# Attention with a feed-forward block behind it: the first feed-forward product begins 11 slots behind the scores instead of 13

## The chip, the cores and the metric

The kernel runs on one core of one Trainium2 chip. The core has five engines that run beside each other, each through its own instructions in order: TensorE (PE, matmuls; PEld is its weight load), VectorE (DVE), ScalarE (ACT), GpSimd (POOL) and SyncE (SP), which in this kernel issues all DMA transfers. They wait for each other through semaphores. The metric is the time of one execution in device microseconds (us), lower is better. The kernel before took 1484.6 us (median of 3 runs, 1483.02 to 1485.44).

## The reference

Attention over 8 batches, 12 heads, 448 positions and a head size of 64, and behind it a feed-forward block with a squared ReLU over the 3584 positions (width 768, inner width 2048). All arrays are float32, or float64 that is read as two words.

```
q_n = q / sqrt(mean(q*q) + 1e-6) * g_q          # k likewise with g_k
scores = q_n @ k_n.T / sqrt(64)
e = exp(scores - max(scores));  attn = e / (sum(e) + 1e-9)
x = attn @ v                                    # heads side by side: 768 columns
h = x @ w_in;  g = s * max(h, 0)**2 + b
out = g @ w_out
```

## The kernel before, in words

**Slots.** The 96 heads are taken as 48 pairs, 6 pairs to a batch. A pair takes 8 slots (two heads, four chunks of keys each), so there are 384 slots, 48 to a batch, and pair p begins in slot 8p. One Python loop walks the slots, and the order in which it emits instructions is the order in which each engine runs them. In slot s TensorE computes the transposed scores of chunk s (L407, L410), the plain scores of chunk s+10 (L369), from which VectorE takes the row maximum (`maximum`, L380), and weighs the values with chunk s-2 (`weigh`, L466). ScalarE takes the exponential of chunk s (L422 or L426), and from pair 12 on it rounds it to a high part (`split_e`, L434), of which VectorE makes the low part of chunk s-1 (`split_e_lo`, L447, tile `al`). The last matmul of a weighing reads that low part. Up to pair 11 the exponential stays in one part and L447 does not occur.

**Fill.** Between these matmuls, six in each slot, stand the matmuls of the first feed-forward product (FFN1) of the batch before (`ffn_in`, L182): 288 matmuls, so exactly 48 slots. They begin START slots after the batch's own 48: with START = 13 the FFN1 of batch 0 fills slots 61 to 108, that of batch 1 slots 109 to 156, and so on. Slots 0 to 60 have no fill. Behind slot 383 the loop runs on for the rest of the fill of batch 6; the FFN1 of batch 7 and the second product (FFN2, L707) follow without attention beside them.

**The way of the sums.** A ones column beside the values makes TensorE deliver the sum of the exponentials with the weighted values. For pair p, counted from its first slot: `take` (slots 6 and 10, ACT L475) copies the result out of PSUM, `gather` (slots 7 and 11, a DMA of 1.8 KB, L483) turns the row of sums into the tile `zt`, `invert` (slot 13, DVE L489 and L490) takes the reciprocal, `divide` step 1 (slot 14) writes it to DRAM, step 2 (slot 16) reads it back onto 64 partitions per head (`zb`), step 3 (slot 18, POOL L507, two instructions) multiplies and leaves the tile `u`. `split_x(b, k)` then rounds `u` of pairs 2k and 2k+1 of the batch into the high part of `x` (ACT L515) and takes the low part (DVE L516): two casts and two subtractions in each of three successive slots, the last of which is the first slot of that batch's fill.

**What stands around it.** `jobs[s]` lists for each slot what else is emitted: loading and normalising q and k of later pairs (L306, L311, L314, L315), scaling them (`scale`, POOL L331 and DVE L332, in slots 1 and 5 of a pair), splitting them (`split_kq`, ACT L350 and L351 in slots 3 and 7, POOL L353 and L354 a slot later), splitting the values (L299, L300). The first nine pairs take another way: rows are normalised and turned on TensorE (`turn`), then split (`split_turned`, ACT L255 to L257 and DVE L259, L260). Functions in `late` (`convert` and `invert`) come at the end of a slot, behind `maximum`. `convert` turns the float64 weights w_in into two float32 parts (ACT L128, L138; DVE L127, L130, L132, L135; POOL L141), piece by piece in slots up to 92. SyncE issues the DMAs in the order of emission too, and waits in that order.

Of the kernel before, what the change touches and what calls it, by code (L numbers as in the profile page):

```python
# [20 lines left out]

LEAST = (1 + 1 / 8) * 2.0 ** (0x70 - 127)

START = 13

AHEAD = 10

# [10 lines left out]
def attention_then_relu2_ffn(  # L38
# [38 lines left out]
    NP = NPAIR // B  # L77
# [15 lines left out]
    W = 8  # L93
# [117 lines left out]
    with tc.tile_pool(name="apool", bufs=1) as ap:  # L211
# [343 lines left out]
        def filler(n):  # L555

            for _ in islice(fill, n):
                pass
# [4 lines left out]
        def at(s_, f, *a):  # L563
            jobs[s_].append((f, a))

        for p in range(NPAIR):
            s0 = W * p
            if p >= NR:
                at(s0 - 32, load, p)
                at(s0 - 28, norm, p)  # L570
                at(s0 - 24, keep, p)
            for j in range(2):
                s1 = s0 + 4 * j
                if p >= NR:
                    at(s1 - 19, load_kq, p, j)
                    at(s1 - 19, spread, p, j)
                    at(s1 - 15, scale, p, j)
                    at(s1 - 13, split_kq, p, j)
                else:
                    at(max(s1 - 28, FIRST), load_rows, p, j)  # L580
                    at(s1 - 20, norm_rows, p, j)
                    at(s1 - 13, turn, p, j)
                    at(s1 - 12, split_turned, p, j)
                at(s1 - 10, double_kb, p, j)
                at(s1 - 6, shift, p, j)
                at(s1 + 6, take, p, j)
                at(s1 + 7, gather, p, j)
            at(s0 - (9 if p >= NV else 5), load_v, p)
            if p >= NV:
                at(s0 - 3, split_v, p)  # L590
            at(s0 + 13, invert, p)
            at(s0 + 14, divide, p, 1)
            at(s0 + 16, divide, p, 2)
            at(s0 + 18, divide, p, 3)
        for b in range(B):
            for k_ in range(3):
                at(W * NP * (b + 1) + START - 2 + k_, split_x, b, k_)
        for _ in range(2):
            at(FIRST + 1, load_piece)
        for s_ in PACE:  # L600
# [12 lines left out]
        with tc.manual_schedule(engines=ORDERED):  # L613
            begun = []
            for s_ in range(FIRST, NSLOT + START + 1):
                if s_ == FIRST:
# [37 lines left out]
                filler(FILL[2])  # L654
                b, m = divmod(s_ + 1 - START, W * NP)
                if m == 0 and b > 0:
# [151 lines left out]
```

## Time and profile before

| | |
|---|---|
| median of 3 runs | 1484.6 us (1483.02 to 1485.44) |
| profiled execution, its own time | 1483.03 us |
| its span (first to last instruction) | 1481.2 us |
| mean granted TensorE clock | 0.997 of full speed |
| busy: PE, PEld | 1443.3 us (97%), 1322.6 us (89%) |
| busy: DVE, ACT, POOL | 862.8 us (58%), 790.5 us (53%), 686.9 us (46%) |

The 1.8 us between the span and the execution's own time lie outside the program's instructions. The shares are means over stages: VectorE is near full in the first 180 us and far from it afterwards. In the 40 slices of the page, TensorE's busy share is 7 tenths in the first slice, 8 in the fourth and the last, and 9 or more in all others.

### The profile page before, as it was taken

Reading aid. Unit: us, or ns where it says so; the run is one execution under the profiler, and the core shown is the slowest. Engines: PE = TensorE matmul, PEld = TensorE weight load, DVE = VectorE, ACT = ScalarE, POOL = GpSimd, SP = SyncE. Lnnn points to the kernel's source line nnn. Section 1 sums busy time; section 2 is a strip of 40 time slices with the busy share of each in tenths; the row PEclk is TensorE's granted clock in tenths of the full one; section 3 lists DMA queues with packets and bytes.
Section 4 is the critical chain, followed back from the end, with each engine's and each line's share of the span. In section 5 each row is a group of like instructions: output and inputs, shape, how many; then the busy total and the mean of one; then the engine's idle time right before and its main releaser. Section 6 shows DMA issues by size and latency. Waiting matters only on the chain. (4 is left out here: it accounts for less than half of the span.)

```text
span 1481.2 us, 21369 instructions
## 1 busy us (share of the span) xinstructions
PE 1443.3 (97%) x7332; PEld 1322.6 (89%) x7332; DVE 862.8 (58%) x1328; ACT 790.5 (53%) x1445; POOL 686.9 (46%) x563
## 2 busy tenths in 40 slices
PE   7998999999999999999999999999999999999998
PEld 6665788899899899899899889999999999999998
DVE  7999996766766666766766664389522222222210
ACT  5777556766766666766766766456322222222210
POOL 7788887777677777777677763100000000000000
PEclk8999999999999999999999999999999999999999
DMA  5456876566666666566666652387333333233200
GB/s 141 130 159 183 233 219 203 171 196 186 188 190 184 189 192 185 170 199 191 188 175 198 189 171 58 118 273 242 105 97 85 96 94 78 79 91 106 79 22 32
DMA packets 218172, 225.31 MB, mean 152 GB/s; under 512 B 77936, under 2 KB 195696, under 8 KB 218064
## 3 DMA queue, kind: packets, MB, share of 16 engines
q1 hardware_dynamic: 218064, 223.95, 51.7%
q8 instruction: 58, 0.95, 0.3%
q14 instruction: 50, 0.41, 0.1%
HBM read 171.71 MB, written 40.82 MB: 143 GB/s over the span
## 5 line engine op out<-in xcount | busy, mean ns | idle before, releaser
L182 PE MATMUL ph<-x,wih 128*128 128x448 f32 x1536 | 490.0, 366 | 1.8 <-DVE x L516 1.8
L182 PEld LDWEIGHTS ph<-x,wih 128*128 128x128 f32 x1536 | 288.7, 188 | 31.7 <-issue 6.4
L380 DVE TENSOR_REDUCE nmx<-sh 112x1 fp32r<-112x448 f32 x384 | 237.0, 620 | 130.7 <-PE sh L369 127.7
L182 PE MATMUL ph<-x,wil 128*128 128x448 f32 x768 | 293.8, 383 | 0.0
L426 ACT ACTIVATE st<-st 128x448 f32<-128x448 f32 (+1 forms) x288 | 151.2, 525 | 220.3 <-PE st L410 213.6
L707 PE MATMUL po<-woh,gh 128*128 128x384 f32 x896 | 228.1, 334 | 0.3 <-ACT r L199 0.3
L707 PE MATMUL po<-wol,gh 128*128 128x384 f32 x896 | 227.9, 334 | 0.0
L707 PE MATMUL po<-woh,gl 128*128 128x384 f32 x896 | 227.7, 334 | 0.0
L466 PE MATMUL av<-ah,vs 128*128 128x448 f32 x576 | 164.3, 366 | 0.1
L369 PE MATMUL sh<-ka,qa 128*112 128x448 f32 x384 | 147.3, 386 | 16.0 <-DVE ka L259 10.9
L707 PEld LDWEIGHTS po<-woh,gh 128*128 128x128 f32 x896 | 161.9, 188 | 0.7 <-ACT r L199 0.6
L707 PEld LDWEIGHTS po<-wol,gh 128*128 128x128 f32 x896 | 161.9, 188 | 0.0
L707 PEld LDWEIGHTS po<-woh,gl 128*128 128x128 f32 x896 | 161.7, 188 | 0.0
L407 PE MATMUL st<-qa,ka 128*128 128x448 f32 (+1 forms) x384 | 159.2, 415 | 1.7 <-ACT e L422 0.8
L182 PEld LDWEIGHTS ph<-x,wil 128*128 128x128 f32 x768 | 144.3, 188 | 17.8 <-issue 6.9
L434 ACT CAST ah<-st 128x448 fp32r<-128x448 f32 (+1 forms) x288 | 153.9, 534 | 1.8
L447 DVE TENSOR_TENSOR al<-st,ah 128x448 fp32r<-128x448 f32 x216 | 132.4, 613 | 35.4 <-ACT ah L434 21.6
L689 ACT ACTIVATE r<-r 128x2048 f32<-128x2048 f32 x28 | 53.7, 1919 | 172.7 <-DMA r<-r_d 172.7
L410 PE MATMUL st<-qb,kb 128*128 128x448 f32 (+1 forms) x384 | 140.2, 365 | 0.0
L690 DVE TENSOR_SCALAR r<-r,sb_s,sb_b 128x2048 f32<-128x2048 f32 x28 | 37.6, 1346 | 173.2 <-ACT r L689 173.2
L507 POOL TENSOR_TENSOR u<-uz,zb 64x448 f32<-64x448 f32 x96 | 115.4, 1203 | 41.4 <-DMA zb<-z_d 27.7
L369 PEld LDWEIGHTS sh<-ka,qa 128*112 128x112 f32 x384 | 107.5, 281 | 28.9 <-ACT wih L138 4.7
(75 smaller groups left out, 2142.1 us busy)
## 6 DMA issues: line engine op xcount, KB each, us to landing
kq<-in_dram SPq DMA_DIRECT2D x78, 448.0 KB, 4.9
rb<-i_d SPq DMA_DIRECT2D x78, 448.0 KB, 5.9
r_d<-r SPq DMA_DIRECT2D x128, 224.0 KB, 2.8
r<-r_d SPq DMA_DIRECT2D x24, 1024.0 KB, 5.9
raw<-in_dram SPq DMA_DIRECT2D x39, 448.0 KB, 5.1
w64i<-in_dram SPq DMA_DIRECT2D x24, 512.0 KB, 4.9
w64o<-in_dram SPq DMA_DIRECT2D x32, 384.0 KB, 4.7
kb<-ka SPq DMA_DIRECT2D x96, 112.0 KB, 3.1
```

The lines of the kernel that those rows point to most:

```text
L182: T.matmul(ph[:, :SEQ], w[:, cc, f0 : f0 + P], xs[b, cc][:, part, :], start=n == 0, stop=n == 3 * NCC - 1,)
L369: T.matmul(sh[:QC, :SEQ], qa[p % 2][:, a].rearrange("k (p c) -> k c p", c=NQ)[:, c], ka[p % 2][:, a], start=True, stop=True,)
L380: V.tensor_reduce(out=nmxs[p][:, c : c + 1], in_=sh[:QC, :SEQ], op=ALU.max, axis=AX.X, negate=True)
L407: T.matmul(st[:rows, :SEQ], ka[n][:, keys], qa[n][:, q], start=True, stop=False)
L410: T.matmul(st[:rows, :SEQ], kb[n][:, keys], qb[n][:, q], start=False, stop=True,)
L426: S.activation(st[:rows, :SEQ], st[:rows, :SEQ], AF.Exp)
L434: S.copy(ah[:rows], sts[i][0][:rows, :SEQ])
L447: V.tensor_tensor(al, st[:rows, :SEQ], ah[:rows].bitcast(F32), ALU.subtract)
L466: T.matmul(av[:, :SEQ], x, a, start=kc == 0 and m == 0, stop=kc == 3 and m == len(todo) - 1,)
L507: G.tensor_tensor(u[a], uzs.pop((p, j))[a], zb[a], ALU.mult)
L689: S.activation(r, r, AF.Square)
L707: T.matmul(po[e][0][:, :HALF], x[:, fc, :], w[:, f, e * HALF : (e + 1) * HALF], start=fc == 0 and m == 0, stop=fc == NFC - 1 and m == 2,)
```

## The change

START goes from 13 to 11: the FFN1 of batch b fills slots 48(b+1)+11 to 48(b+1)+58, two slots earlier, and the loop ends two slots earlier. `split_x` goes with it, since its slots are counted from START. `invert` and the three steps of `divide` come one slot earlier in each pair (12, 13, 15, 17 instead of 13, 14, 16, 18); `take` and `gather` stay. For batch 0 alone, `split_x` of pairs 0 and 1 is put in slot 27 and that of pairs 2 and 3 in slot 43; pairs 4 and 5 stay in slot 59.

```diff
--- before.py
+++ after.py
@@ -21,7 +21,7 @@
 
 LEAST = (1 + 1 / 8) * 2.0 ** (0x70 - 127)
 
-START = 13
+START = 11
 
 AHEAD = 10
 
@@ -588,13 +588,14 @@
             at(s0 - (9 if p >= NV else 5), load_v, p)
             if p >= NV:
                 at(s0 - 3, split_v, p)
-            at(s0 + 13, invert, p)
-            at(s0 + 14, divide, p, 1)
-            at(s0 + 16, divide, p, 2)
-            at(s0 + 18, divide, p, 3)
+            at(s0 + 12, invert, p)
+            at(s0 + 13, divide, p, 1)
+            at(s0 + 15, divide, p, 2)
+            at(s0 + 17, divide, p, 3)
         for b in range(B):
             for k_ in range(3):
-                at(W * NP * (b + 1) + START - 2 + k_, split_x, b, k_)
+                s1 = W * NP * (b + 1) + START - 2 + k_
+                at(s1 if b else min(s1, 2 * W * (k_ + 1) + 11), split_x, b, k_)
         for _ in range(2):
             at(FIRST + 1, load_piece)
         for s_ in PACE:
```

On VectorE, at the end of batch 2, whose `x` is split here: `x2_0` to `x2_5` are the six tiles, `al152` is the low part of chunk 152, `sh163` the plain scores of chunk 163, `kq21_0` is scaled for pair 21. Before, from slot 153 on:

```order
L332 SCALAR_TENSOR_TENSOR kq21_0_4099<-kq21_0_4099,gqk_200,rb21_0_4101 128x448
L447 TENSOR_TENSOR al152_4221<-st152_4175,ah152_4208 128x448
L380 TENSOR_REDUCE nmx20_4139<-sh163_4217 112x1
L447 TENSOR_TENSOR al153_4250<-st153_4203,ah153_4234 128x448
L380 TENSOR_REDUCE nmx20_4139<-sh164_4244 112x1
L516 TENSOR_TENSOR x2_0_4271<-u12_3124,x2_0_4271 128x448
L516 TENSOR_TENSOR x2_1_4274<-u13_3348,x2_1_4274 128x448
L447 TENSOR_TENSOR al154_4281<-st154_4228,ah154_4264 128x448
L380 TENSOR_REDUCE nmx20_4139<-sh165_4277 112x1
L516 TENSOR_TENSOR x2_2_4300<-u14_3569,x2_2_4300 128x448
L516 TENSOR_TENSOR x2_3_4303<-u15_3792,x2_3_4303 128x448
L447 TENSOR_TENSOR ah155_4294<-st155_4259,ah155_4294 64x448
```

and now:

```order
L332 SCALAR_TENSOR_TENSOR kq21_0_4115<-kq21_0_4115,gqk_200,rb21_0_4117 128x448
L516 TENSOR_TENSOR x2_0_4236<-u12_3112,x2_0_4236 128x448
L516 TENSOR_TENSOR x2_1_4239<-u13_3335,x2_1_4239 128x448
L447 TENSOR_TENSOR al152_4246<-st152_4191,ah152_4223 128x448
L380 TENSOR_REDUCE nmx20_4155<-sh163_4242 112x1
L516 TENSOR_TENSOR x2_2_4265<-u14_3559,x2_2_4265 128x448
L516 TENSOR_TENSOR x2_3_4268<-u15_3780,x2_3_4268 128x448
L447 TENSOR_TENSOR al153_4275<-st153_4218,ah153_4258 128x448
L380 TENSOR_REDUCE nmx20_4155<-sh164_4271 112x1
L516 TENSOR_TENSOR x2_4_4296<-u16_4003,x2_4_4296 128x448
L516 TENSOR_TENSOR x2_5_4299<-u17_4227,x2_5_4299 128x448
L447 TENSOR_TENSOR al154_4308<-st154_4253,ah154_4290 128x448
```

The first two subtractions of `x` now stand in slot 153, ahead of `al152`, where none stood, and the last two stand in slot 155, ahead of `al154`, where the first two stood.

On GpSimd in the same slots, with `u17` the result of pair 17, the last of batch 2. Before:

```order
L354 TENSOR_TENSOR qb0_190<-kq20_1_3990,qa0_186 64x448
L331 TENSOR_TENSOR kq21_0_4099<-kq21_0_4099,rb21_0_4101 128x448
L507 TENSOR_TENSOR u17_4237<-uz17_0_3905,zb17_4186 64x448
L507 TENSOR_TENSOR u17_4237<-uz17_1_4019,zb17_4186 64x448
L353 TENSOR_TENSOR ka1_185<-kq21_0_4099,ka1_185 64x448
```

and now:

```order
L354 TENSOR_TENSOR qb0_190<-kq20_1_4008,qa0_186 64x448
L507 TENSOR_TENSOR u17_4227<-uz17_0_3920,zb17_4171 64x448
L507 TENSOR_TENSOR u17_4227<-uz17_1_4032,zb17_4171 64x448
L331 TENSOR_TENSOR kq21_0_4115<-kq21_0_4115,rb21_0_4117 128x448
L353 TENSOR_TENSOR ka1_185<-kq21_0_4115,ka1_185 64x448
```

The two multiplications of `u17` went ahead of the scaling of `kq21_0`.

On VectorE in the first batch, with `zt3` the sums of pair 3, `tk6` the turned rows of pair 6 and `w64i9` a piece of w_in. Before, from the maximum of chunk 46 on:

```order
L380 TENSOR_REDUCE nmx5_1034<-sh46_1159 112x1
L127 TENSOR_SCALAR wai9_1162<-w64i9_1008 128x512
L130 SCALAR_TENSOR_TENSOR wai9_1162<-w64i9_1008,wai9_1162 128x512
L259 TENSOR_TENSOR ka0_184<-tk6_0_0_1132,ka0_184 64x448
L260 SCALAR_TENSOR_TENSOR qb0_190<-tk6_0_1_1137,gqk_200,qa0_186 64x448
L235 TENSOR_REDUCE ssq7_0_1174<-sq7_0_1155 112x8
L380 TENSOR_REDUCE nmx5_1034<-sh47_1176 112x1
L489 TENSOR_SCALAR zt3_1029<-zt3_1029 128x7
L490 RECIPROCAL zt3_1029<-zt3_1029 128x7
```

and now:

```order
L380 TENSOR_REDUCE nmx5_1040<-sh46_1165 112x1
L489 TENSOR_SCALAR zt3_1035<-zt3_1035 128x7
L490 RECIPROCAL zt3_1035<-zt3_1035 128x7
L127 TENSOR_SCALAR wai9_1170<-w64i9_1017 128x512
L130 SCALAR_TENSOR_TENSOR wai9_1170<-w64i9_1017,wai9_1170 128x512
L259 TENSOR_TENSOR ka0_184<-tk6_0_0_1138,ka0_184 64x448
L260 SCALAR_TENSOR_TENSOR qb0_190<-tk6_0_1_1143,gqk_200,qa0_186 64x448
L235 TENSOR_REDUCE ssq7_0_1182<-sq7_0_1161 112x8
L380 TENSOR_REDUCE nmx5_1040<-sh47_1185 112x1
```

The reciprocal of `zt3` went from behind the maximum of chunk 47 to behind that of chunk 46; the conversion of the weights and the split of pair 6 (`ka0`, `qb0`) now stand behind it.

## Rows read from the trace of the kernel before

**Rows 1.** Windows: stretch, us, busy PE, PEld, DVE, ACT, POOL, clock, DMA
```profile
100.00:120.00 20.00, 17.71 (x77) 11.98 (x76) 18.61 (x31) 16.43 (x33) 17.58 (x16) 1.00 0.54 142
...
160.00:180.00 20.00, 20.00 (x86) 16.06 (x85) 19.86 (x27) 11.97 (x23) 16.38 (x12) 1.00 0.82 229
...
900.00:1000.00 100.00, 100.00 (x494) 92.25 (x494) 56.86 (x117) 50.15 (x94) 11.59 (x10) 1.00 0.49 161
```

**Rows 2.** Waits of TensorE: who waited for whom, us in total, times, longest
```profile
PE av L466 <- DVE al L447: 11.0, 12, 1.0
...
PE sh L369 <- DVE ka L259: 10.9, 8, 2.4
```

**Rows 3.** Timeline of PE, its score matmuls of slots 144, 152 and 160: start, us, what
```profile
350.23 0.36 PE L410 MATMUL st<-qb,kb 128*128 128x448 f32 x1
...
369.38 0.36 PE L410 MATMUL st<-qb,kb 128*128 128x448 f32 x1
...
391.13 0.36 PE L410 MATMUL st<-qb,kb 128*128 128x448 f32 x1
```

**Rows 4.** Timeline of PE, the last weighing matmul in slots 154, 156 and 158
```profile
375.69 0.37 PE L466 MATMUL av<-al,vs 128*128 128x448 f32 x1
...
381.70 0.47 PE L466 MATMUL av<-al,vs 128*128 128x448 f32 x1 [0.96 <-DVE al L447]
...
387.77 0.47 PE L466 MATMUL av<-al,vs 128*128 128x448 f32 x1 [0.86 <-DVE al L447]
```

**Rows 5.** Timeline of VectorE (DVE), slots 153 to 157
```profile
370.93 1.30 DVE L332 SCALAR_TENSOR_TENSOR kq<-kq,gqk,rb 128x448 f32<-128x448 f32 x1
...
378.87 2.24 DVE L516 TENSOR_TENSOR x<-u,x 128x448 fp32r<-128x448 f32 x2 [3.17 <-ACT x L515]
...
381.03 0.61 DVE L447 TENSOR_TENSOR al<-st,ah 128x448 fp32r<-128x448 f32 x1
...
386.03 1.16 DVE L516 TENSOR_TENSOR x<-u,x 128x448 fp32r<-128x448 f32 x2
```

**Rows 6.** Timeline of GpSimd (POOL), slots 152 to 156
```profile
371.65 1.59 POOL L331 TENSOR_TENSOR kq<-kq,rb 128x448 f32<-128x448 f32 x1
...
373.21 2.38 POOL L507 TENSOR_TENSOR u<-uz,zb 64x448 f32<-64x448 f32 x2
...
379.21 1.42 POOL L354 TENSOR_TENSOR qb<-kq,qa 64x448 fp32r<-64x448 f32 x1
```

**Rows 7.** Timeline of ScalarE (ACT), slots 153 and 155
```profile
372.23 0.53 ACT L426 ACTIVATE st<-st 128x448 f32<-128x448 f32 x1 [1.36 <-PE st L410]
...
378.27 1.04 ACT L515 CAST x<-u 128x448 fp32r<-128x448 f32 x2
```

**Rows 8.** Timeline of VectorE in the first batch, sums of pairs 3 and 5
```profile
91.95 0.62 DVE L380 TENSOR_REDUCE nmx<-sh 112x1 fp32r<-112x448 f32 x1 [0.74 <-PE sh L369]
...
122.20 0.62 DVE L380 TENSOR_REDUCE nmx<-sh 112x1 fp32r<-112x448 f32 x1
...
126.19 1.09 DVE L311 TENSOR_REDUCE ssq<-raw 128x14 f32<-128x896 f32 x1 [1.09 <-ACT raw L306]
```

**Rows 9.** Timeline of SyncE (SPq), the gather of the sums of pairs 3 and 5
```profile
91.41 0.47 SPq L483 DMA_DIRECT2D zt<-uz  x1
...
122.50 0.55 SPq L483 DMA_DIRECT2D zt<-uz  x1
```

**Rows 10.** DMA issues around 91.4 and 122.5 us: count, KB each, us to landing
```profile
zt<-uz SPq DMA_DIRECT2D x1, 1.8 KB, 3.5
...
zt<-uz SPq DMA_DIRECT2D x1, 1.8 KB, 5.4
```

**Rows 11.** Timelines of PE in slot 43 and of POOL, the division of pair 3
```profile
103.53 0.37 PE L410 MATMUL st<-qb,kb 128*128 128x448 f32 x1
...
108.26 2.36 POOL L507 TENSOR_TENSOR u<-uz,zb 64x448 f32<-64x448 f32 x2
```

**Rows 12.** Timeline of GpSimd at the end, the division of the last pair
```profile
949.37 2.66 POOL L507 TENSOR_TENSOR u<-uz,zb 64x448 f32<-64x448 f32 x2 [10.18 <-ACT r L199]
```

## The prediction

> **What bounds the kernel now.** I read the windows first, then the waits of TensorE, then the timelines of the places these name. TensorE is the bound, but not everywhere. At the end, from 900 to 1000 us, where the last slots and the fill alone run, it is busy all of 100 us; from 100 to 120 us, in the slots without fill, it is busy 17.71 of 20 us, and VectorE 18.61; from 160 to 180 us, with fill, VectorE is busy 19.86 of 20 [rows 1]. The number of matmuls stays, so the change can only win or lose what TensorE waits, and that lies in two places.
>
> The first is the end of each batch. TensorE waits 12 times for the low part of the exponentials, 11.0 us in all, longest 1.0 [rows 2]. These are two waits at each of six batch ends (batches 1 to 6). Eight slots without such a wait take 369.38 - 350.23 = 19.15 us, the next eight, with the split of x in them, 391.13 - 369.38 = 21.75 [rows 3]. A batch end costs 2.60 us, six of them 15.6 us. In slot 156 TensorE waited 0.96 us, in slot 158 it waited 0.86 [rows 4]; shared out in proportion, 1.37 and 1.23 us with the restart behind each.
>
> The second is the first batch, where VectorE runs late and TensorE waits 8 times, 10.9 us, for its split of the turned rows [rows 2].
>
> **The two slots of fill.** Eight slots hold 94 matmuls (24 of scores, 22 of weighing, 48 of fill), 19.15 / 94 = 0.204 us each. Two slots of fill are 12 matmuls, 2.44 us. They leave the end, where TensorE never waits, and so shorten it by 2.44 us. They enter slots 59 and 60. If VectorE sets the pace there and for the next 20 slots, as 19.86 of 20 us says, they go into time in which TensorE would wait and cost nothing; if TensorE sets it, they cost 2.44 again. So the term is between -2.44 and 0; I take -2.44, as the row at 160 to 180 us is the nearest.
>
> **The ends of batches 1 to 6.** Pairs 4 and 5 now split in slot 155 (of batch 2), where pairs 0 and 1 did, behind the same casts of ScalarE and beside the same GpSimd work. In the trace two subtractions took 2.24 us there and 1.16 in slot 157 [rows 5], where GpSimd's subtraction of q, 1.42 us from 379.21, runs beside the first [rows 6]. That wait stays: 1.37. Slot 157 loses its subtractions and becomes an ordinary one of its kind, in which TensorE does not wait: the 1.23 goes (between 0 and 0.3 left, since VectorE comes out of slot 155 late; I take 0.1).
>
> New is slot 153. There the low part of chunk 152 must be there at 375.69 [rows 4]. VectorE is through with its scaling at 370.93 + 1.30 = 372.23 [rows 5]. ScalarE ends the exponential at 372.23 + 0.53 = 372.76, and two casts take 1.04 [rows 7], so the first x is there at 373.3 and the second at 373.8. With two subtractions at their quick 1.16 and the low part at 0.61, the latter is done at 375.1, in time: 0 lost. But GpSimd's two multiplications by the sums, 2.38 us from 373.21 in the trace [rows 6], now start in place of the scaling at 371.65, and the scaling, 1.59 us, follows, so GpSimd works through to about 375.6. With the slow 2.24 of slot 155 the low part is done at 373.3 + 2.24 + 0.61 = 376.15, 0.46 late, 0.6 with the restart. If each subtraction first waits out one GpSimd instruction (1.19 and 1.59), it is done at 377.8 less the overlap, some 1.5 late. Between 0 and 1.5 I take 0.6, the row of slot 155, which has the same neighbours.
>
> A batch end then costs 0.6 + 1.37 + 0.1 = 2.07 instead of 2.60: six times 0.53, -3.2 us. The bounds are 1.37 (-7.4 us) and 3.2 (+3.6 us).
>
> The Trainium skill (SBUF — State Buffer, "SBUF: two separate sides") says that GpSimd and a VectorE instruction with two SBUF inputs share one port pair under an exclusive lock, and that the loser waits for the whole instruction. The 2.24 against 1.16 us agrees. By that rule alone every subtraction in slot 153 waits once and the batch end comes to about 3.0; this is the second rival below.
>
> **The reciprocal a slot earlier.** On VectorE it waits for the gather, which has not moved. For pair 3 it will stand behind a maximum that ends at 91.95 + 0.62 = 92.57 [rows 8]; the gather was issued at 91.41 [rows 9] and landed 3.5 us later [rows 10], at 94.9. VectorE waits 2.3 us, and behind it in its order stand the conversion of weights and the split of turned rows for which TensorE waits. For pair 5: 122.82 against 122.50 + 5.4 = 127.9, 5.1 us, of which 1.09 is idle today anyway [rows 8 to 10]. By then VectorE runs some 3.5 us later (2.3 and one pair of subtractions, 1.16). If what these 1.8 KB wait for in their queue (loads, I assume) does not get later with it, the wait shrinks to 1.6; between 0 and 4.0. The other early pairs I take at nothing; from pair 9 on I assume that the low parts come early enough to cover the waits. Together +3.9 us, between 2.3 and 6.3.
>
> **The split of pairs 0 to 3 in slots 27 and 43.** Four casts and four subtractions leave slots 59 and 60. VectorE does the same work in the same late stretch: 0, with 2.24 - 1.16 = 1.1 us for each pair of subtractions either way, so -2.2 to +2.2. ScalarE in slot 43 waits, if the result of pair 3 is late: rival three.
>
> **The end.** The chain of the last pair is one slot shorter in count and loses two slots of 1.22 us. Its division ended at 949.37 + 2.66 = 952.03 [rows 12]. Its way back to DRAM no longer stands behind a store of the fill, so it comes earlier too. Nothing, up to +1.
>
> **Sum.** -2.44 - 3.2 + 3.9 + 0 + 0 = -1.7 us against the profiled execution's 1483.0 (its span 1481.2 and 1.8 around it), which lies 1.6 under the median of 1484.6. Against the median: 1482.9 us.
>
> **The rivals.** *No wait in slot 153.* The casts reach VectorE in the gap between two GpSimd instructions and both subtractions take 1.16. For it: the 1.16 of slot 157 [rows 5]. Against it: GpSimd now has three instructions in a row there. The batch ends cost 1.47, six times -1.1 = -6.8; with -2.44 + 3.9 that is -5.3: 1479.3 us.
>
> *The wait of slot 158 only moves to slot 154.* Each subtraction waits for a GpSimd instruction, a batch end costs about 3.0, six times +0.4 = +2.4, with +1.5 from the first batch: 1488.5 us, slower. It decides once the low part of chunk 152 comes over 1.1 us late.
>
> *The first batch loses more than it gains.* In slot 43 ScalarE must cast pair 3, whose division ran at 108.26 to 110.62, while TensorE began that slot's exponential at 103.53 [rows 11]. A slot earlier is some 1.8 us: 108.8, about 4 us after ScalarE gets there, and the exponentials queued behind reach TensorE two slots on, some 3 us: 1 to 4 us lost, the same again in slot 27, and the full 4.0 for pair 5. With +2 for each slot, +2.4 for pair 5 and the rest as forecast, 1482.9 + 6.4 = 1489.3 us. Against it: GpSimd may get to the division sooner than one slot, if it was its inputs that held it; no row decides that.
>
> **Chances.** About 0.2% (3 us) is what a measurement can tell from no change. Forecast 0.44 (its own range 1479.5 to 1486), no wait 0.20, the moved wait 0.14, the first batch 0.22. Faster by over 3 us: 0.15 of the forecast's 0.44, 0.18 of the second, 0.02 from the others: 0.35. Slower by over 3 us: 0.04 + 0.10 + 0.15 = 0.29. Within: 0.36. The range runs from the first rival less 2 to the slower ones: 1477.3 to 1490.
>
> **What will show it.** The waits for the low part at six batch ends: in the slots 154 and 156 of batch 2, none in slot 158; eight slots in about 21.2 us instead of 21.75. A wait of `zt` for its gather on VectorE in the first batch, 2 us at pair 3. No wait of TensorE after 900 us. I am wrong if slot 154 has no wait or one over 1.1 us, if `zt` waits under 1 us in all, or if ScalarE's casts in slots 27 and 43 stand and wait for `u`.

## The result, and the profile after

The changed kernel took 1498.84 us (median of 4 runs, 1497.77 to 1501.08) against 1484.57 (4 runs): a ratio of 1.0099, 95% interval 1.0082 to 1.0117. Forecast was 1482.9, with a range up to 1490.0. It is slower by 14.3 us, and the forecast had it faster by 1.7.

Where the time went is read from TensorE's score matmul of a slot (L410) in both profiled executions (spans 1481.2 and 1496.0):

| slot | before, us | after, us | difference |
|---|---|---|---|
| 0 | 27.25 | 28.14 | +0.9 |
| 59 | 134.65 | 146.42 | +11.8 |
| 62 | 140.60 | 155.73 | +15.1 |
| 80 | 191.19 | 202.05 | +10.9 |
| 112 | 273.64 | 287.90 | +14.3 |
| 376 | 918.13 | 934.80 | +16.7 |
| end of the span | 1481.2 | 1496.0 | +14.8 |

The end gave 1.9 back, as it should with two slots less behind slot 383. The ends of batches 2 to 6 (slots 112 to 376) lost 2.4; that of batch 1, just before slot 112, costs about what it did. The rest was lost before slot 112: 10.9 us between slots 0 and 59, and 3.4 from slot 80 to 112. From slot 59, where the fill now enters, to slot 80 the change gains 0.9.

The windows that answer to [rows 1], and short ones in the first batch; columns as there:

```profile
100.00:120.00 20.00, 16.48 (x73) 11.28 (x71) 18.12 (x33) 16.62 (x32) 13.46 (x14) 1.00 0.53 147
160.00:180.00 20.00, 20.00 (x88) 16.29 (x87) 16.13 (x24) 9.84 (x20) 17.04 (x15) 1.00 0.86 253
900.00:1000.00 100.00, 100.00 (x491) 91.51 (x491) 51.89 (x104) 48.98 (x101) 20.34 (x18) 1.00 0.45 147
...
90.00:95.00 5.00, 2.86 (x8) 1.48 (x7) 4.94 (x8) 2.15 (x5) 3.71 (x4) 0.84 0.14 46
95.00:100.00 5.00, 5.00 (x22) 3.89 (x21) 1.95 (x4) 2.55 (x6) 4.34 (x5) 0.82 0.50 142
...
130.00:135.00 5.00, 1.92 (x8) 1.13 (x6) 1.18 (x5) 3.64 (x7) 4.38 (x5) 0.94 0.91 263
135.00:140.00 5.00, 3.71 (x11) 2.60 (x12) 4.47 (x7) 0.92 (x2) 1.98 (x2) 0.50 0.57 151
```

VectorE (the third busy time of a line) did not become fuller. It is emptier, 18.12 instead of 18.61 and 16.13 instead of 19.86 of 20 us, and from 130 to 135 it is busy 1.18 of 5. TensorE (the first) is busy 1.92 there, and the granted clock of the next window is 0.50.

VectorE at the reciprocals of pairs 3 and 5, which answers to [rows 8]:

```profile
100.57 0.17 DVE L489 TENSOR_SCALAR zt<-zt 128x7 f32<-128x7 f32 x1 [1.31 <-DMA zt<-uz]
...
130.13 0.62 DVE L380 TENSOR_REDUCE nmx<-sh 112x1 fp32r<-112x448 f32 x1
134.54 0.17 DVE L489 TENSOR_SCALAR zt<-zt 128x7 f32<-128x7 f32 x1 [3.78 <-DMA zt<-uz]
134.74 0.20 DVE L490 RECIPROCAL zt<-zt 128x7 f32<-128x7 f32 x1
134.86 0.64 DVE L132 SCALAR_TENSOR_TENSOR wai<-w64i,wai 128x512 int32<-128x512 int32 x1
135.53 0.62 DVE L259 TENSOR_TENSOR ka<-tk,ka 64x448 fp32r<-64x448 f32 x1
```

SyncE issued the gather of pair 5 at 130.16, and it landed 4.4 us later:

```profile
130.16 0.55 SPq L483 DMA_DIRECT2D zt<-uz  x1
```

```profile
zt<-uz SPq DMA_DIRECT2D x1, 1.8 KB, 4.4
```

And TensorE in the same stretch:

```profile
131.00 0.71 PE L407 MATMUL st<-qa,ka 128*128 128x448 f32 x1
131.55 0.37 PE L410 MATMUL st<-qb,kb 128*128 128x448 f32 x1
136.29 0.70 PE L369 MATMUL sh<-ka,qa 128*112 128x448 f32 x1 [4.37 <-DVE ka L259]
136.79 1.70 PE L466 MATMUL av<-e,vf 128*128 128x448 f32 x2
137.61 1.25 PE L407 MATMUL st<-qa,ka 128*128 128x448 f32 x1
```

A DMA of 1.8 KB that is late by 3.78 us makes VectorE late with the split `ka`, and TensorE waits 4.37 us for it. Its matmuls then take longer: that of L407, which took 0.71 us ahead of the wait, takes 1.25.

Between slots 80 and 112 the waits of pairs 9 and 10 (1.75 and 2.74 us) stand ahead of maxima, and TensorE waits 0.91 and 1.82 us for these. The second of them:

```profile
239.16 2.87 DVE L489 TENSOR_SCALAR zt<-zt 128x7 f32<-128x7 f32 x1 [2.74 <-DMA zt<-uz]
```

```profile
244.42 0.56 PE L369 MATMUL sh<-ka,qa 128*112 128x448 f32 x1 [1.82 <-DVE nmx L380]
```

TensorE's waits as a whole, which answer to [rows 2]:

```profile
PE sh L369 <- DVE ka L259: 14.0, 7, 4.4
PE av L466 <- DVE al L447: 13.2, 18, 1.1
```

The batch end of batch 2, which answers to [rows 3 to 6]: eight slots without a split take 383.64 - 364.50 = 19.14 us, the next eight 406.02 - 383.64 = 22.38, so it costs 3.24 instead of 2.60. First TensorE, then VectorE and GpSimd in slot 153:

```profile
364.50 0.36 PE L410 MATMUL st<-qb,kb 128*128 128x448 f32 x1
383.64 0.36 PE L410 MATMUL st<-qb,kb 128*128 128x448 f32 x1
391.24 0.47 PE L466 MATMUL av<-al,vs 128*128 128x448 f32 x1 [1.11 <-DVE al L447]
397.36 0.47 PE L466 MATMUL av<-al,vs 128*128 128x448 f32 x1 [0.96 <-DVE al L447]
406.02 0.37 PE L410 MATMUL st<-qb,kb 128*128 128x448 f32 x1
```

```profile
387.53 3.12 DVE L516 TENSOR_TENSOR x<-u,x 128x448 fp32r<-128x448 f32 x2 [1.10 <-ACT x L515]
390.58 0.61 DVE L447 TENSOR_TENSOR al<-st,ah 128x448 fp32r<-128x448 f32 x1
```

```profile
385.91 2.76 POOL L507 TENSOR_TENSOR u<-uz,zb 64x448 f32<-64x448 f32 x2
388.75 1.42 POOL L331 TENSOR_TENSOR kq<-kq,rb 128x448 f32<-128x448 f32 x1
```

The two subtractions of slot 153 took 3.12 us, with GpSimd's three instructions beside them, against 1.16 when quick and 2.24 in slot 155 [rows 5]. In slots 154 and 156 TensorE waits 1.11 and 0.96. A third wait, 0.34 in slot 158, is just above the 0 to 0.3 that the prediction left there.

### The profile page after: what moved, and what is told of

Same layout as the page of the kernel before. It is cut to its first block, busy times and chain, and to the rows that moved or that the text cites. A ratio compares the mean times of both kernels' runs of the same rounds, so it can differ in the third digit from the quotient of the medians.

```text
span 1496.0 us, 21391 instructions
## 1 busy us (share of the span) xinstructions
PE 1448.3 (97%) x7332; PEld 1326.1 (89%) x7332; DVE 866.0 (58%) x1328; ACT 789.8 (53%) x1445; POOL 672.6 (45%) x563
## 4 chain that ended last, share of the span: by engine, by line
PE 85%; DVE 7%; issue 3%; DMA 2%; ACT 2%; POOL 0%; SPq 0%; DVEq 0%; ACTq 0%; POOLq 0%
PE po L708 31%; PE ph L182 27%; PE av L466 13%; PE sh L369 5%; PE st L407 4%; PE st L410 4%; DVE x L516 1%; DMA zt<-uz 1%; DVE nmx L380 1%; PE tk L247 1%; DVE al L447 1%; DMA w64i<-in_dram 1%; DVE kq L332 1%; DVE wai L130 1%; DVE zt L489 1%
## 5 line engine op out<-in xcount | busy, mean ns | idle before, releaser
L407 PE MATMUL st<-qa,ka 128*128 128x448 f32 (+1 forms) x384 | 160.0, 417 | 0.0
L507 POOL TENSOR_TENSOR u<-uz,zb 64x448 f32<-64x448 f32 x96 | 124.8, 1300 | 44.1 <-DMA zb<-z_d 40.3
L410 PE MATMUL st<-qb,kb 128*128 128x448 f32 (+1 forms) x384 | 140.8, 367 | 0.0
```

The lines of the kernel that those rows point to most:

```text
L407: T.matmul(st[:rows, :SEQ], ka[n][:, keys], qa[n][:, q], start=True, stop=False)
L410: T.matmul(st[:rows, :SEQ], kb[n][:, keys], qb[n][:, q], start=False, stop=True,)
L507: G.tensor_tensor(u[a], uzs.pop((p, j))[a], zb[a], ALU.mult)
```

## The experiments

All were timed beside the kernel before on the same chip, in five rounds; its median there was 1483.8 to 1484.1 us. Every run's ratio to it stands with its 95% interval. The edits are shown cut to the lines that matter; comments in them are added.

**The parts one by one.** Three kernels each do one part of the change, and a fourth the whole change with the old offsets of the sums for pairs 0 to 11.

```diff
 e1_sums_alone (START 13, split_x as before)
-            at(s0 + 13, invert, p)   # divide 14, 16, 18
+            at(s0 + 12, invert, p)   # divide 13, 15, 17
 e2_start_alone
-START = 13
+START = 11
 e3_x_alone (START 13, sums as before)
+                at(s1 if b else min(s1, 2 * W * (k_ + 1) + 11), split_x, b, k_)
 e4_late_sums_first (the changed kernel)
+            lag = 1 if p < 2 * NP else 0
+            at(s0 + lag + 12, invert, p)   # divide lag + 13, 15, 17
```

> Only the way of the sums is a slot shorter; START stays 13 and x is split where it was. Theory A (VectorE stands and waits for the gathers of the first twelve pairs, and TensorE behind it): most of the loss is here, TensorE's waits for ka grow as in the changed kernel (14.0 us and more) and the time is 1494 to 1500 us. Theory B (the loss comes from splitting x in slots 27 and 43, or from the fill entering early): within 3 us of 1484.6.

> Only START goes to 11, and the splitting of x with it, also for batch 0; the sums keep their old offsets. Theory A: the two slots of fill leave the end (-2.44 us) and are mostly absorbed in the first batch; the batch ends move by +0.6 at most each; 1481 to 1485 us. Theory B: the fill enters where VectorE is full and the first batch loses; 1489 us or more.

> Only the splitting of batch 0 moves: pairs 0 and 1 to slot 27, 2 and 3 to slot 43, 4 and 5 to slot 59; START 13 and the old way of the sums. Theory A: the same work in the same stretch, within 2 us of 1484.6. Theory B: the casts stand and wait for u or push the exponentials back, 1488 us or more.

> The changed kernel, but the pairs of the first two batches keep the old offsets of the sums (invert in slot 13); all later pairs have the new ones. Theory A: the 12.9 us lost by slot 64 go, the first batch stands near the kernel before or up to 4 us ahead of it, and the time is 1480 to 1486 us. Theory B: 1493 us or more.

| run | us | ratio |
|---|---|---|
| e1_sums_alone | 1512.47 | 1.0187 (1.0174 to 1.0200) |
| e2_start_alone | 1485.00 | 1.0007 (0.9997 to 1.0017) |
| e3_x_alone | 1488.99 | 1.0033 (1.0020 to 1.0046) |
| e4_late_sums_first | 1490.08 | 1.0037 (1.0025 to 1.0049) |

Theory A named the right part, the sums, but missed three of the four numbers. The sums alone cost 28.4 us, twice the whole change: 13.4 in the profile by slot 64 (beyond what it was behind at slot 0), the rest at batch ends, where with START 13 TensorE's waits for `al` grew to 18.3 us (12 of them, longest 2.1). So the parts do not add up. With START 13 the last splits of batch 1 stand in slot 109. There the reciprocal of the next pair, a slot earlier now, comes ahead of them and of the `al` that TensorE waits for; before it came behind that `al`, at 270.67. TensorE's wait for this `al` is 2.09 us, where it was 0.86 in [rows 4]:

```profile
283.43 1.09 DVE L489 TENSOR_SCALAR zt<-zt 128x7 f32<-128x7 f32 x1
```

START 11 takes the splits out of that slot.

START alone came out at the edge of theory A. Its profiled execution, 2.4 us above its median, loses 5.2 us between slots 59 and 80. The two slots of fill have entered there, and TensorE waits longer for `x` (4.2 us; 1.8 before, 1.3 in the change):

```profile
PE ph L182 <- DVE x L516: 4.2, 3, 3.1
```

The early splits cost where theory A said nothing would. Slot 27 of the run with x alone, ScalarE and then GpSimd:

```profile
81.65 0.56 ACT L515 CAST x<-u 128x448 fp32r<-128x448 f32 x1 [4.69 <-POOL u L507]
```

```profile
79.29 2.33 POOL L507 TENSOR_TENSOR u<-uz,zb 64x448 f32<-64x448 f32 x2
```

GpSimd reaches the multiplication of pair 1, emitted in slot 26, only at 79.29, when slot 29 has begun (79.11). In the kernel before it came no sooner, at 78.41, but nobody waited for it then. Now the cast finds no `u`: ScalarE stands 4.69 us in slot 27 and 4.58 in slot 43, with the exponentials queued behind. e4_late_sums_first, between what the two theories gave it, has the early splits and the old offsets for pairs 1 and 3 together, and the same two waits, 9.0 us in all. In the change itself GpSimd takes up that multiplication at 74.64 and no cast waits.

**The waits taken away.** In the first of two kernels the reciprocal is taken of a constant tile (the division by the sums is left out); in the second the gather goes out a slot earlier.

```diff
 e5_no_gather_wait (the changed kernel)
-            V.tensor_scalar(zt, zt, 1e-9, None, ALU.add)
-            V.reciprocal(zt, zt)
+            V.tensor_scalar(zr, zone, 1e-9, None, ALU.add)
+            V.reciprocal(zr, zr)    # zone: a tile of ones; divide 1 then writes zr
 e6_gather_with_take (the changed kernel)
-                at(s1 + 7, gather, p, j)
+                at(s1 + 6, gather, p, j)
```

> The changed kernel, but the reciprocal of slot 12 is taken of a constant tile of ones and sent on in place of the gathered sums (the division by the sums is left out of the result; the gather is still issued, nobody waits for it; instruction counts the same). Theory A (VectorE standing for the gather is what the first batch loses): the zt waits, 22 us in all, are gone, slot 64 comes within 4 us of the kernel before instead of 12.9, and the time is 1484 to 1490 us. Theory C (the loss is in where the steps stand, in the casts of x in slots 27 and 43 or in the queue of SyncE, not in this wait): 1495 us or more.

> The changed kernel with the gather issued in the same slot as take (6 and 10 instead of 7 and 11); results as before. Theory A: the gather lands up to one early slot (1.4 to 3 us) sooner, the waits of zt in the first batch fall from 9.4 us to under 5, and the time is 1486 to 1493 us. Theory C: no change, 1496 to 1501 us; or SyncE, which now waits for take with its loads queued behind, makes it slower.

Without the waits: 1491.02 us, 1.0048 (1.0034 to 1.0061), 7.8 less than the change, and just beyond theory A. The waits go with half of the loss and not all of it. They are not VectorE's alone: SyncE writes the reciprocal to DRAM and waits in order too, 10.7 us before these writes from 40 to 140 us in the change and 6.8 in this run, and no run tells the two shares apart. Issuing the gather earlier gave nothing, as theory C had it: 1498.81, 1.0098 (1.0085 to 1.0112). The wait of pair 5 fell only from 3.78 to 2.61 us and that of pair 3 went, but slot 64 stood where it had (13.7 behind before, of which 1.2 at slot 0). At pair 5 TensorE still waited 3.55 us, and the clock behind it was again 0.50.

What was left in the run without waits shows in slots 27 to 31 (lines are two higher there: L518 is the subtraction):

```profile
78.24 2.22 DVE L518 TENSOR_TENSOR x<-u,x 128x448 fp32r<-128x448 f32 x2
...
82.36 1.29 DVE L135 SCALAR_TENSOR_TENSOR wai<-wih,wai 128x512 f32<-128x512 f32 x1
83.69 0.62 DVE L259 TENSOR_TENSOR ka<-tk,ka 64x448 fp32r<-64x448 f32 x1
```

```profile
84.46 0.70 PE L369 MATMUL sh<-ka,qa 128*112 128x448 f32 x1 [2.73 <-ACT wih L138]
```

The view names a cast of ScalarE as releaser; but the matmul reads `ka`, which was done only at 83.69 + 0.62 = 84.31. The split of the turned rows stood behind the subtractions and what they had pushed back.

**The parts in pairs.** START and sums without the early split; the same without the waits; then the old offsets for pairs 0 to 5 alone, and for pairs 6 to 11 alone.

```diff
 e9_start_and_sums (the changed kernel); e10_start_sums_no_wait has e5's edit too
-                at(s1 if b else min(s1, 2 * W * (k_ + 1) + 11), split_x, b, k_)
+                at(W * NP * (b + 1) + START - 2 + k_, split_x, b, k_)
 e13_first_six_late (e9 with)
+            lag = 1 if p < NP else 0
 e14_second_six_late (e9 with)
+            lag = 1 if NP <= p < 2 * NP else 0
```

> The change without its third part: START 11 and the shorter way of the sums, x of batch 0 split in slots 57 to 59. If the gather waits are the larger part of the first batch's loss: they stay, and the time is 1494 to 1500 us. If the splitting in slots 27 and 43 is the larger part: under 1492 us.

> As the run before, and the reciprocal is taken of a constant tile of ones, so that VectorE waits for no gather (the division by the sums is left out of the result). If the gather wait and the early splitting together are all that the first batch loses: it stands where the run with START alone stands, 1483 to 1487 us. If something else in the shorter way of the sums costs too: 1489 us or more.

> START 11 and the shorter way of the sums without the early splitting (1497.0 us), but pairs 0 to 5 keep the old offsets of the sums. If the waits of the first batch (pairs 3 and 5 above all) are the larger part of the 7.8 us that the waits cost: 1489 to 1493 us. If the waits of pairs 6 to 11, in slots 60 to 100, are: 1494 us or more.

> The same, but pairs 6 to 11 keep the old offsets and pairs 0 to 5 have the new ones. If the waits of the first batch are the larger part: 1493 us or more, near 1497.0. If those of pairs 6 to 11 are: 1489 to 1493 us, and the jumps in slots 86 to 100 are gone.

| run | us | ratio |
|---|---|---|
| e9_start_and_sums | 1496.96 | 1.0100 (1.0081 to 1.0118) |
| e10_start_sums_no_wait | 1489.15 | 1.0041 (1.0028 to 1.0055) |
| e13_first_six_late | 1484.88 | 1.0003 (0.9994 to 1.0012) |
| e14_second_six_late | 1495.66 | 1.0086 (1.0071 to 1.0102) |

By the medians the early split adds 1498.84 - 1496.96 = 1.9 us to the other two parts, but the ratios are alike, 1.0099 and 1.0100, so it is not told from nothing. The waits again make 7.8 (1496.96 - 1489.15); in the profiles the two kernels differ by 8.2 at slot 59, beyond what they were behind at slot 0. With the old offsets for the first six pairs alone the loss is gone (1484.88, 12.1 less, and below what was expected of it), with those for the next six hardly any of it is (1.3 less), although VectorE's waits for gathers stay longer in the run that is fast:

```profile
DVE zt L489 <- DMA zt<-uz: 17.6, 11, 6.1
```

That is the run with the first six late; with the second six late it is

```profile
DVE zt L489 <- DMA zt<-uz: 14.9, 7, 6.1
```

The 17.6 us lie at pairs 6 and later, 6.1 of them at the last pair, where the kernel before waits 5.6 too. They cost little: the run is as fast as the one with START alone, though its profile loses 2.0 us between slots 80 and 100. Of the 14.9, 2.90 and 4.31 lie at pairs 3 and 5, and cost most. A wait is worth what stands behind it: the splits of turned rows on VectorE end in slot 56 (12 slots ahead of the second half of pair 8, the last to be turned), so they stand behind the reciprocals of pairs 0 to 5, in slots 12 to 52, and of no later pair.

**The rest of 4 us.** 12.1 less 7.8 leaves 4.3 that is no wait for a gather. Two more kernels without the waits put steps of `divide` back.

```diff
 e15_division_late (e10 with)
-            at(s0 + 17, divide, p, 3)
+            at(s0 + 18, divide, p, 3)
 e16_reciprocal_early_alone (e15 with)
-            at(s0 + 13, divide, p, 1)   # and 15, divide 2
+            at(s0 + 14, divide, p, 1)   # and 16, divide 2
```

> The run with START and sums without the wait (1489.2 us; the reciprocal of a constant tile, the division by the sums left out of the result), but step 3 of divide, GpSimd's two multiplications, stands in slot 18 again. In that run GpSimd stood 2.5 and 2.9 us in the first batch for the sums' way back from DRAM before these multiplications. If that is what is left of the first batch's loss beside the waits: 1484 to 1486.5 us. If not: 1488 us or more.

> The same, and steps 1 and 2 of divide in slots 14 and 16 again, so that only the reciprocal (of the constant tile) stands a slot earlier. It should be as the run with START alone, 1483.5 to 1486.5 us, whichever step it is; 1488 us or more would mean that the reciprocal's place on VectorE costs without any wait.

With the multiplication back in slot 18: 1485.29 us, 1.0014 (1.0006 to 1.0023), 3.9 less, as expected, but not by the waits that the expectation names. Those are followed by nothing that lasts: at slot 59 the two profiles stand within 0.1 us of each other, and at slot 80 they are 4.2 apart. What costs is pair 5. In e10_start_sums_no_wait GpSimd stands for its sums' way back from DRAM, and the scaling of `kq` (L331) has got behind the multiplication (L509 in these two kernels). ScalarE's cast of `kq` waits for that scaling, the casts of `x` (L517) stand behind it, and the fill's first matmuls wait for `x`. First GpSimd, then ScalarE and TensorE:

```profile
137.51 3.78 POOL L509 TENSOR_TENSOR u<-uz,zb 64x448 f32<-64x448 f32 x2 [2.93 <-DMA zb<-z_d]
141.37 1.13 POOL L331 TENSOR_TENSOR kq<-kq,rb 128x448 f32<-128x448 f32 x1
```

```profile
142.53 0.56 ACT L350 CAST ka<-kq 128x448 fp32r<-128x448 f32 x1 [4.50 <-POOL kq L331]
144.08 0.59 PE L182 MATMUL ph<-x,wih 128*128 128x448 f32 x1 [2.99 <-ACT x L517]
```

With the multiplication back, the scaling goes first, at 134.66, and no wait of TensorE for `x` is over 0.4 us there:

```profile
134.66 1.65 POOL L331 TENSOR_TENSOR kq<-kq,rb 128x448 f32<-128x448 f32 x1 [0.18 <-DMA rb<-i_d]
```

The last run missed its expectation a little: 1487.30, 1.0028 (1.0017 to 1.0039). Its nine runs reach from 1484.06 to 1491.97 and those of the other from 1482.76 to 1487.96, so the two overlap, and I make nothing of the difference.

**A better version.** Three slots later the early splits would find their `u`, and the subtractions need not stand ahead of `al` at all.

```diff
 e7_x_early_with_slack (START 11, sums as before)
+                at(s1 if b else min(s1, 2 * W * (k_ + 1) + 14), split_x, b, k_)
 e8_subtract_late (the kernel before; e11 is e7 with it, e12 the changed kernel with it)
                 S.copy(x[:, 0, :], u)
-                V.tensor_tensor(x[:, 1, :], u, x[:, 0, :].bitcast(F32), ALU.subtract)
+                halves.append((x, u))
+        def rest_x(b, k):
+            while halves:
+                x, u = halves.pop(0)
+                V.tensor_tensor(x[:, 1, :], u, x[:, 0, :].bitcast(F32), ALU.subtract)
-        late = (convert, invert)
+        late = (convert, invert, rest_x)
+                at(W * NP * (b + 1) + START - 2 + k_, rest_x, b, k_)
```

> START 11, the old offsets of the sums everywhere, and the splitting of batch 0 three slots later than in the change: pairs 0 and 1 in slot 30, 2 and 3 in slot 46. In the run with x alone ScalarE stood 4.7 and 4.6 us for u in slots 27 and 43. If it was that wait that cost: no such wait, no loss at slots 31 and 47, the fill enters with less in its way, 1480 to 1484 us. If the casts and subtractions themselves cost there: 1487 us or more.

> The kernel before (START 13, old offsets), but the two subtractions of split_x stand at the end of their slot on VectorE, behind al and the maximum, instead of ahead of al. If a batch end's 2.60 us come from al standing behind the subtractions: the 12 waits for al (11.0 us) go to under 4 us, eight slots with the split take 19.2 to 19.9 us instead of 21.75, and the time is 1470 to 1476 us. If the casts of ScalarE ahead of ah, or GpSimd, hold al up as well: 1478 us or more.

> The best parts together: START 11, old offsets of the sums, x of batch 0 split in slots 30 and 46, and all subtractions of x at the end of their slot, behind al and the maximum. With -2.44 us at the end, batch ends of 0.5 instead of 2.6 and a first batch like that of the run in slots 30 and 46: 1467 to 1471 us, under the 1471.5 of late subtractions alone. If START 11 finds al late in these slots in another way: 1472 us or more.

> The changed kernel with all subtractions of x at the end of their slot. If its batch ends are al standing behind the subtractions: six times 2.3 to 2.9 us go, TensorE's waits for al fall from 13.2 us to under 4, the first batch's loss stays (12 to 14 us at slot 64): 1482 to 1487 us. If GpSimd's three instructions in a row hold al up in another way: 1490 us or more.

| run | us | ratio |
|---|---|---|
| e7_x_early_with_slack | 1485.73 | 1.0012 (1.0003 to 1.0021) |
| e8_subtract_late | 1471.51 | 0.9915 (0.9902 to 0.9929) |
| e11_slack_subtract_late | 1466.72 | 0.9883 (0.9867 to 0.9898) |
| e12_change_subtract_late | 1485.10 | 1.0006 (0.9997 to 1.0015) |

In e7_x_early_with_slack no cast of slots 30 and 46 waits for `u`. Its profile is 2.8 us behind at slot 35 and level again at slot 80, beyond the 0.5 it had at slot 0; what made it miss its 1480 to 1484 us are 3.3 us lost between there and slot 368, at the batch ends.

The other three came out as expected, the best version a little under its range. The late subtractions are worth 12.3 us on the kernel before, 13.7 on the changed one and 19.0 on that one. TensorE's waits for `al`, 11.0 us before [rows 2], are 2.4 in e8_subtract_late:

```profile
PE av L466 <- DVE al L447: 2.4, 6, 0.4
```

VectorE in slots 155 and 156 of it (L523 is the subtraction): still 2.25 us for the pair, but behind `al` and the maximum; TensorE waits for the `al` after them once in a batch end, 0.4 us:

```profile
374.90 0.62 DVE L447 TENSOR_TENSOR al<-st,ah 128x448 fp32r<-128x448 f32 x1 [0.64 <-ACT ah L434]
376.07 0.62 DVE L380 TENSOR_REDUCE nmx<-sh 112x1 fp32r<-112x448 f32 x1 [0.55 <-PE sh L369]
377.42 2.25 DVE L523 TENSOR_TENSOR x<-u,x 128x448 fp32r<-128x448 f32 x2 [0.72 <-ACT x L515]
379.69 0.62 DVE L447 TENSOR_TENSOR ah<-st,ah 64x448 fp32r<-64x448 f32 x1
```

The best version, e11_slack_subtract_late, has nothing left of the batch end: slots 152 and 160 start at 367.46 and 386.60, 19.14 us apart.

```profile
367.46 0.36 PE L410 MATMUL st<-qb,kb 128*128 128x448 f32 x1
...
386.60 0.36 PE L410 MATMUL st<-qb,kb 128*128 128x448 f32 x1
```

## Why the prediction was wrong, step by step

By their medians the runs share the 14.7 us between 1484.1 and 1498.8 out like this: START alone +0.9, the shorter sums of pairs 6 and later -0.1 (1484.88 less 1485.00), those of pairs 0 to 5 +12.1, the early split +1.9; together 14.8. (Beside the change itself the kernel before took 1484.57, so the loss there is 14.3.) The medians are not that sharp. The runs of START and sums lie at 1496.2 to 1497.0 and at 1501.6 to 1502.2, and by the ratios (1.0100 less 1.0003) pairs 0 to 5 come to 14 us and the early split to nothing.

- *The two slots of fill* (-2.44). The end gave 1.9. What they cost where they enter was put at 0, and from slot 59 to 80 the change gains 0.9, so the step held there. It does not hold everywhere: in the profile of START alone these slots lose 5.2 us, about the 2.44 of the matmuls themselves and the 2.4 by which the fill waits longer for `x`, which the prediction does not name. The step also rested on half a row: the same line of [rows 1] that shows VectorE at 19.86 of 20 us shows TensorE at 20.00.
- *The ends of batches 1 to 6* (-3.2). This step failed too: they lost about 2.4, of which START alone has 2.0 in its profile. The rival in which the wait of slot 158 only moves to slot 154 was right: it named 1.1 us late as the point from which it decides, and TensorE waited 1.11. I took 0.6 from slot 155 because its neighbours on GpSimd seemed the same; there one GpSimd instruction and the end of another ran beside the pair, in slot 153 three in a row. The Trainium skill (SBUF — State Buffer, "SBUF: two separate sides") has the loser of the shared port wait out the whole instruction. With 3.12 us for the pair the trace agrees with that better than with my middle value. At the ends of batches 1 and 4 the wait was 0.42 and 0.43 with the same order: there the pair began 0.69 us behind GpSimd's first multiplication and took 2.43 and 2.44, at the other four 1.62 behind and took 3.1.
- *The reciprocal a slot earlier* (+3.9, at most 6.3). This is the step that failed most. The forecast found the places, pairs 3 and 5, where VectorE waited 5.1 us instead of 3.9. Pair 3 waited 1.31 instead of 2.3. Pair 5 was given 1.6, on the guess that the gather would not get later with VectorE; it waited 3.78, because take, gather and loads all moved with the late slots. Then it took VectorE's wait for TensorE's loss. In the profile TensorE waited 4.37 us behind pair 5 and worked on at half its clock. Runs with and without the waits differ by 7.8. For pairs 9 and later the prediction assumed that low parts cover the waits; pairs 9 to 11 have none, the waits came, and TensorE lost 0.91 and 1.82 us to two of them.
- *The steps behind the reciprocal* were priced at nothing. In the kernels without gather waits GpSimd's multiplication a slot earlier, which waits for DRAM ahead of the scaling of `kq`, is worth 3.9 us (1489.15 less 1485.29); in the profiles it goes where the fill enters. The prediction saw this division only as something that comes earlier for the casts. How much of the 3.9 is in the change, which gains between slots 59 and 80, no run shows.
- *The split of pairs 0 to 3* (0, within 2.2 either way) came to between 0 and 1.9, inside its bounds. The rival had the casts waiting for `u`: that is what the split does alone (+4.9), but not in the change.
- *The last pair's way* (0): TensorE has no wait behind 900 us, as forecast.

So the sum missed by 16.0, from -1.7 to +14.3. By the medians 8.2 of it lie on the first six pairs' sums (12.1 instead of 3.9), 5.6 on the batch ends, 0.5 on the end and up to 1.9 on the early split; closer than that the medians cannot tell. The third rival had the right side and place, and pair 5's wait nearly right (4.0 for 3.78), but it put the rest on casts that did not wait.

## What to carry to other kernels

An instruction that waits belongs behind those that others wait for: moving two subtractions behind the one that TensorE needs was worth 12 us, where the change that shortened the chain around them lost 14. Before you shorten a chain by moving its steps earlier, ask how long anybody waits for its end (here TensorE for `x`, 1.8 us before), and for each step what stands behind it on its engine: a step whose input is not there yet holds all of that up. And a wait on a side engine is charged by what stands behind it, not by its length: of 17.6 us of waits for gathers at pairs 6 and later hardly anything shows in the time, while those of pairs 3 and 5, 5.1 us in the changed kernel, go with half of the loss.

## What the hardware showed

- TensorE's clock. Granted was 1.00 from 25 us on in the kernel before, in all 27 rows of 5 us up to 160 us, with waits of up to 1.7 us in that stretch. In the changed kernel it was 0.84 and 0.82 from 90 to 100 us, where TensorE had waited 2.14 us (behind a wait of 2.33 us at 84.07 it stayed 1.00), and behind the wait of 4.37 us it was 0.50 from 135 to 140 us, the lower of its two levels (1.2 of 2.4 GHz); there L410 took 0.58 instead of 0.37 us and two weighing matmuls 1.70 instead of 0.91. Over the whole run the same 7332 matmuls were busy 1448.3 us instead of 1443.3; how much of these 5.0 us is clock, no run tells apart.
- The start. In the profiled change TensorE was already 0.9 us behind at slot 0, where the change has done nothing yet. From 25 to 30 us the clock was 0.64, in the kernel before 1.00. Other kernels here show the same (e1_sums_alone 0.55 and 1.1 us behind, e6_gather_with_take 0.59 and 1.2), so it is no part of the change.
- The same two subtractions on VectorE took 1.16, 2.24, 3.12 or, beside four GpSimd instructions (150.60 in the changed kernel), 4.57 us. The 1.16 of slot 157 [rows 5] was not without a neighbour either. There VectorE's scaling (385.44) began just ahead of GpSimd's, and it was GpSimd that took longer, 2.71 us where the median of this instruction is 1.16:

```profile
385.47 2.71 POOL L331 TENSOR_TENSOR kq<-kq,rb 128x448 f32<-128x448 f32 x1
```
